# Attention stage of one core: VectorE's maxima, scale chain and half differences of the next head pair stand in other thirds of its ticks

## The chip, the cores and the metric

The kernel runs on one core of one Trainium2 chip, as one launch. The metric is the device time of a launch in microseconds (us); the kernel before takes 2028.98 us, the median of three runs.

## What is computed

Block-causal attention over q, k, v of shape (4, 8, 576, 64), then a mixture of eight experts, then a gated layer:

```python
scores = scale * np.matmul(q, k.transpose(0, 1, 3, 2))
mask = (pos // 64)[:, None] >= (pos // 64)[None, :]
attn = softmax(np.where(mask, scores, -1e9))
x = np.matmul(attn, v)            # then to (2304, 512)
# 8 rounds of row and column scaling of exp(x @ w_gate) give P
x = sum(P[:, e:e+1] * (np.maximum(x @ w1[e], 0) @ w2[e]) for e in range(8))
out = (silu(x @ wg) * (x @ wv)) @ wo
```

All is float32 on the outside. Inside, an operand is scaled by a power of two and cut into two float16 halves, a high one and the difference that is left, so that a product is made of float16 matmuls.

## The kernel before, in words

Two heads make a pair; there are 16 pairs p (four batches of four), and the work of a pair is cut into eight ticks u = 0 to 7 (`NTK`, `TICKS`, L824 to L827), in which the score rows of one, or two, blocks of 64 queries are made. `attention` (L833) is a generator. One pass of its loop (L1216) is one tick tk = 8p + u, and it yields three times, so that a tick has three thirds; between them the caller (L1417) puts in other work at fixed rates: the first two experts' weights (`w0`, in the first part of the stage), and, once the first batch is through, `fill`, which is router, expert products and their evacuation.

- Third 0: the events of the tick (below), then the scores' matmuls of the tick (`scores`, L989), in a PSUM bank of a pool of three.
- Third 1: the transposes of tick tk-4 (L1067, L1076), pending sums of x (`work`), the reciprocals of tick tk-2 (`normalise`, L1034 to L1039, after which GpSimd scales the rows, L1044), and VectorE's row maxima of the tick's own scores (`maxima`, L1002).
- Third 2: ScalarE's exponentials of tick tk-1 (`exps`, L1019).

The order is written out by hand: each engine executes in the order in which this loop issues, and tiles carry the semaphores. A next pair is prepared by events, a table from tick to functions (`at`, L1174). With r = 8p the first tick of pair p, and i = 0 for q, 1 for k, the pairs from 4 on have:

- `load_qk` (L907): SP's load of q or k into the tile `qk0` or `qk1`, at r-14 and r-13. Each has one buffer, which `lo_qk` of the pair before is the last to read.
- `max_qk` (L920): VectorE's maximum (L923), r-11 and r-10; after k's, two products that make `qk_d` (L103).
- `across_mid` (L106) at r-8: a matmul that spreads the maxima over the partitions into a bank that it shares with the scores of tick u = 0.
- `scale_qk` (L929) at r-7: VectorE's read of that bank (L116), and then the chain of the scales: L156, L163, L164 and two of L934.
- `hi_qk` (L937): ScalarE's high half (L940), r-6 and r-4; `lo_qk` (L942): VectorE's difference (L944), which reads that half, r-5 and r-4, and behind each on SP four transfers that put the halves into the scores' layout (`st`, L955 and L957).

The maxima of v for the next batch (`scan_max`, L883) are VectorE events too, one per pair. In each tick all these events stand in third 0, ahead of the tick's reciprocals and row maxima.

Of the kernel before, what the change touches and what calls it, by code (L numbers as in the profile page):

```python
# [30 lines left out]
def attention_moe_glu_kernel(  # L31
# [66 lines left out]
    def across_begin(mx, n, name):  # L98
        pool = pairs[0] if name[0] in "qv" else small
        tag = "dgw" if name[0] == "w" else f"dg{n}"  # L100
        d = pool.tile([P, n, P], F32, tag=tag, name=f"{name}_d", bufs=1)
        for i in range(n):
            nc.vector.tensor_scalar_mul(d[:, i], ident, mx[:, i : i + 1])  # L103
        return {"d": d, "n": n, "name": name}

    def across_mid(g):  # L106
        bank, g["free"] = spread[0](g["name"])
        n = g["n"]
        g["row"] = bank[:, : n * P].rearrange("p (n q) -> p n q", n=n)
        nc.tensor.matmul(  # L110
            bank[:, : n * P], ones, g["d"].rearrange("p n q -> p (n q)"), start=True, stop=True
        )

    def across_end(g):
        r = small.tile([P, g["n"]], F32, tag=f"sr{g['n']}", name=f"{g['name']}_r")
        nc.vector.tensor_reduce(r, g["row"], axis=AX.X, op=ALU.max)  # L116
        g["free"]()
        row_out[0] = False
        return r
# [23 lines left out]

        return made

    def pow2_end(g, n, top, name, root=False, s=None, inv=None):

        given[0] += 340
        r = across_end(g)
        e = small.tile([P, n], F32, tag=f"se{n}", name=f"{name}_e")  # L150
        if root:
            nc.vector.tensor_scalar(
                e.bitcast(I32), r.bitcast(I32), 1, EXPONENT, op0=ALU.logical_shift_right, op1=ALU.bitwise_and
            )
        else:
            nc.vector.tensor_single_scalar(e.bitcast(I32), r.bitcast(I32), EXPONENT, op=ALU.bitwise_and)  # L156
        if inv is None:
            inv = small.tile([P, n], F32, tag=f"si{n}", name=f"{name}_i")
        if s is None:
            s = small.tile([P, n], F32, tag=f"ss{n}", name=f"{name}_s")  # L160
        up = 64 if root else 0
        least = 2.0 ** ((-50 if root else -100) - top)
        nc.vector.tensor_scalar(inv, e, 2.0 ** (up - top), least, op0=ALU.mult, op1=ALU.max)  # L163
        nc.vector.reciprocal(s, inv)  # L164
        return s, inv
# [661 lines left out]
    NTK = len(TICKS)  # L827
    ORDER = (0, 2, 1, 3)
# [4 lines left out]
    def attention(actx):  # L833
# [17 lines left out]
        vs, vmx, vt, qk, st, et, xf = {}, {}, {}, {}, {}, {}, {}  # L851
# [11 lines left out]
        def where(p):  # L863
            return p // NPAIR, ORDER[p % NPAIR]
# [3 lines left out]
        def load_v(b, hp, tag, bufs=1):  # L868
            t = tag
            if isinstance(tag, str):  # L870
                t = ap.tile([P, NJ, P], F32, tag=tag, name=f"{tag}_{b}_{hp}", bufs=bufs)
            cols = slice(hp * P, (hp + 1) * P)
            nc.gpsimd.memset(t[S - nf * P :, nf], 0.0)
            nc.sync.dma_start(t[:, :nf], v[b, : nf * P, cols].rearrange("(j p) d -> p j d", p=P))
            nc.sync.dma_start(t[: S - nf * P, nf], v[b, nf * P :, cols])
            return t
# [43 lines left out]
        def max_qk(p, i):  # L920
# [5 lines left out]
            if i == 1:  # L926
                st[p]["m"] = across_begin(st[p]["m"], 2, f"qk{p}")

        def scale_qk(p):  # L929
            s, iv = pow2_end(st[p]["m"], 2, 11, f"qk{p}")  # L930
            sc = small.tile([P, 2], F32, tag="sc", name=f"sc_{p}")
            for i in range(2):
                f = (1 - 2 * i) * D**-0.5
                nc.vector.tensor_scalar(sc[:, i : i + 1], iv[:, 0:1], iv[:, 1:2], f, op0=ALU.mult, op1=ALU.mult)  # L934
            st[p].update(sc=sc[:, 0:1], nsc=sc[:, 1:2], s=s)
# [143 lines left out]
        def rest(p):  # L1079

            t = ps_x.tile([P, 512], F32, tag="x", name=f"t_{p}_r").rearrange("p (j q) -> p j q", q=P)
            return self_transpose(p, NC - 1, 4, t)

        def values(p, grp):
            g = st[p]
            c0, c1 = (0, 4) if grp == 0 else (4, NC)
            a = g["a0"] if grp == 0 else g["a1"]
            nj = (c1 + 1) // 2
            n = (c1 - c0) * CB
            x = ps_x.tile([P, 512], F32, tag="x", name=f"x_{p}_{grp}")[:, :n]  # L1090
            for j in range(nj):
                f = max(c0, 2 * j)
                for h in range(2):
                    nc.tensor.matmul(
                        x[h * D : (h + 1) * D, (f - c0) * CB : n],
                        vt[p][:, j, h * D : (h + 1) * D],
                        a[:, j, f - c0 : c1 - c0, h * CB : (h + 1) * CB],
                        start=j == 0,
                        stop=j == nj - 1,
                    )  # L1100
            return x
# [59 lines left out]
        def work(n):  # L1161
            for _ in range(min(n, len(pend))):
                pend.popleft()()

        def hurried():
            if hurry[0]:
                work(1)
                hurry[0] -= 1
                if not hurry[0]:
                    ready[0] += S // 2  # L1170

        events = {}

        def at(tick, f, *a):  # L1174
            events.setdefault(tick, []).append(lambda: f(*a))

        for p in range(1, npairs):
            r = p * NTK
            if p < DIRECT:
                if p > 1:  # L1180
                    at(r - NTK, load_direct, p)
                    at(r - 2, lambda p: vt.update({p: load_v(*where(p), "v", 2)}), p)
                continue
            for i in range(2):
                if p > 1:
                    at(r - 14 + 1 * i, load_qk, p, i)
                at(r - 11 + i, max_qk, p, i)
                at(r - 6 + 2 * i, hi_qk, p, i)
                at(r - 5 + 1 * i, lo_qk, p, i)
            at(r - 8, lambda p: across_mid(st[p]["m"]), p)  # L1190
            at(r - 7, scale_qk, p)
            at(r - 2, lambda p: vt.update({p: load_v(*where(p), "v", 2)}), p)
        for b in range(B):
            r = (b - 1) * NPAIR * NTK
            for i in range(NPAIR):
                if b:
                    at(r + i * NTK + (0 if i else 3), scan_load, b, i)
                at(r + i * NTK + NTK if b else 1 + i, scan_max, b, i if b else ORDER[i])
            r = r + NPAIR * NTK if b else NPAIR
            at(r, scale_v_begin, b)  # L1200
            at(r + (2 if b else 1), lambda b: across_mid(vmx[b]), b)
            at(r + (3 if b else 2), scale_v_end, b)
# [10 lines left out]
        def on(k):  # L1213
            return 0 <= k < tot

        for tk in range(tot + NTK):  # L1216
            p, u = divmod(tk, NTK)
            calm[0] = 0 < u < 5
            here[0] = (p, u) if on(tk) else None
            for f in events.pop(tk, ()):  # L1220
                f()
            here[0] = None
            if on(tk):
                scores(p, u)
            if u == 6 and p < npairs:
                take(p, 0, values(p, 0))
            hurried()
            yield
            out1 = None
            if on(tk - 4):  # L1230
                out1 = transposes(*divmod(tk - 4, NTK))
            if hurry[0]:
                hurried()
            else:
                work(2 if len(pend) > 6 else 1)
            if on(tk - 2):
                normalise(*divmod(tk - 2, NTK))
            if out1:
                out1()
            if on(tk):  # L1240
                maxima(p, u)
            yield

            if p and u == 4:
                work(len(pend))
                take(p - 1, 1, values(p - 1, 1))
                st.pop(p - 1)
                vt.pop(p - 1)
                if p == npairs:
                    work(len(pend))  # L1250
                    ready[0] = B * S // 2
                elif p % NPAIR == 0:
                    hurry[0] = len(pend)
            if p and u == 3:
                rest(p - 1)()
            if on(tk - 1):
                exps(*divmod(tk - 1, NTK))
            if u != 4:
                hurried()
            yield  # L1260


# [619 lines left out]
```

## Time and profile before

| what | us |
|---|---|
| median of three runs | 2028.98 |
| lowest run | 2028.92 |
| profiled execution, its own time | 2025.01 |
| span of its trace, first to last instruction | 2023.2 |

All numbers of the trace come from the one profiled execution. "Busy" counts an engine's instructions from start to end; PE is TensorE's matmuls, PEld its weight loads, DVE is VectorE, ACT is ScalarE, POOL is GpSimd and SPq the queue of SyncE, from which most transfers are issued. A row of the timeline has a start, a length, the engine, the line, what is written and read, a count (rows of equal instructions are merged), and in square brackets how long the engine was idle before it and what ended that. Tick ends are read off VectorE's rows of L1002, whose last part is a `DVE_READ_ACCUMULATOR2`. Attention with its fill stands in about the first 340 us of the span.

### The profile page before, as it was taken

To read this page: it belongs to the slowest core of one execution; us is meant where nothing else is said; L and a number is where in the kernel's file an instruction comes from. 1 tells how busy PE (TensorE), PEld (TensorE's weight loads), DVE (VectorE), ACT (ScalarE), POOL (GpSimd) and SP (SyncE) were. 2 spreads that over 40 slices of the span, in tenths; PEclk is the share of its full clock that TensorE was granted. 3 is DMA by queue.
4 is the path that set the end of the run, shared out by engine and by line. 5 is a ranking of instruction groups with operands and counts; after the bars stand their busy time and mean duration, and the time that the engine had idled before them with its cause. 6 is when DMAs were issued, how large, how long until landed. Compare 5 with 4: busy or idle time off the path is not lost. (4 is left out here: it accounts for less than half of the span.)

```text
span 2023.2 us, 47049 instructions
## 1 busy us (share of the span) xinstructions
PE 1940.9 (96%) x18378; PEld 1669.3 (83%) x18378; DVE 1593.5 (79%) x3404; ACT 1383.8 (68%) x2880; POOL 622.4 (31%) x876
## 2 busy tenths in 40 slices
PE   8789999999999999989999999999999889999998
PEld 4457677889888988878888888898889778888987
DVE  8886774888889788798978889778886887667666
ACT  6766775477777788777877877778776656544443
POOL 5544444013333333333333333333332132000000
PEclk9899999999999999999999999999999999999999
DMA  5334331326777786777767767677686100301111
GB/s 154 110 104 116 112 89 39 131 59 134 154 170 165 147 171 129 168 154 162 171 133 166 158 136 176 132 165 158 143 178 152 38 12 17 95 1 53 33 43 53
DMA packets 168079, 236.72 MB, mean 117 GB/s; under 512 B 16432, under 2 KB 84656, under 8 KB 167856
## 3 DMA queue, kind: packets, MB, share of 16 engines
q0 software_dynamic: 67136, 108.29, 31.0%
q1 hardware_dynamic: 100720, 125.42, 19.6%
q8 instruction: 144, 2.36, 0.5%
q14 instruction: 79, 0.65, 0.1%
HBM read 90.39 MB, written 24.38 MB: 57 GB/s over the span
## 5 line engine op out<-in xcount | busy, mean ns | idle before, releaser
L548 PEld LDWEIGHTS <-w 128*128 128x128 f16 x6720 | 609.3, 98 | 81.1 <-issue 17.5
L658 PEld LDWEIGHTS <-m_h 128*128 128x128 f16 x5292 | 512.9, 98 | 69.5 <-issue 6.7
L1537 POOL DMA_DIRECT2D acc<-ev x354 | 311.9, 928 | 577.3 <-ACT ev L1541 393.4
L548 PE MATMUL abc_m_b<-xs,w 128*128 128x256 f16 (+1 forms) x3840 | 474.9, 263 | 7.8 <-ACT m_t L575 4.8
L658 PE MATMUL m_o_b<-w,m_h 128*128 128x256 f16 x3024 | 403.3, 273 | 9.8 <-ACT ev L1541 6.0
L658 PE MATMUL m_o_ac<-w,m_h 128*128 128x256 f16 x2268 | 309.4, 273 | 0.0
L548 PE MATMUL abc_m_c<-xs,w 128*128 128x256 f16 (+1 forms) x1920 | 227.7, 263 | 0.0
L1541 ACT ACTIVATE ev<-m_o_b,pe 128x256 f32<-128x256 f32 x354 | 163.8, 479 | 66.7 <-PE m_o_b L658 45.4
L1541 ACT ACTIVATE ev<-m_o_ac,pe 128x256 f32<-128x256 f32 x236 | 136.3, 581 | 45.2 <-PE m_o_ac L658 43.8
L183 DVE SCALAR_TENSOR_TENSOR w<-wr,ws,w 128x512 f16<-128x512 f32 x210 | 156.0, 752 | 8.3 <-ACT w L179 8.3
L179 ACT ACTIVATE w<-wr,ws 128x512 f16<-128x512 f32 x210 | 150.1, 724 | 16.5 <-DVE ws L164 11.4
L194 DVE TENSOR_TENSOR m_h<-m_t,m_h 128x512 f16<-128x512 f32 x189 | 129.5, 687 | 32.4 <-ACT m_h L696 31.5
L696 ACT CAST m_h<-m_t 128x512 f16<-128x512 f32 x189 | 117.1, 619 | 29.1 <-DVE m_t L720 28.0
L689 ACT ACTIVATE m_h<-m_t 128x512 f16<-128x512 f32 x189 | 118.3, 626 | 23.0 <-DVE m_t L587 14.9
L548 PEld LDWEIGHTS <-gg_w 128*128 128x128 f16 x1260 | 114.4, 98 | 22.0 <-issue 10.0
L693 DVE SCALAR_TENSOR_TENSOR m_h<-m_t,m_h 128x512 f16<-128x512 f32 x189 | 128.6, 685 | 3.1 <-ACT m_h L689 2.8
L1524 POOL DMA_DIRECT2D acc<-ev_s x52 | 62.5, 1201 | 218.8 <-ACT ev_s L1517 214.1
L548 PEld LDWEIGHTS <-gv_w 128*128 128x128 f16 x1260 | 113.9, 98 | 15.1 <-issue 3.5
L658 PEld LDWEIGHTS <-g_h 128*128 128x128 f16 x1134 | 111.6, 99 | 16.3 <-issue 2.3
L1044 POOL TENSOR_SCALAR e<-e,r 128x64 f32<-128x64 f32 (+2 forms) x144 | 85.0, 597 | 118.5 <-DVE r L1039 78.7
L548 PE MATMUL abc_m_a<-xs,w 128*128 128x256 f16 (+1 forms) x960 | 118.5, 263 | 0.0
L572 DVE TENSOR_TENSOR m_t<-m_t,abc_m_b 128x512 f32<-128x512 f32 x73 | 49.4, 677 | 68.3 <-PE abc_m_b L548 60.3
(320 smaller groups left out, 3393.4 us busy)
## 6 DMA issues: line engine op xcount, KB each, us to landing
acc<-ev POOLq DMA_DIRECT2D x354, 256.0 KB, 4.1
wr<-in_w_dram SPq DMA_DIRECT2D x128, 256.0 KB, 5.5
acc<-ev_s POOLq DMA_DIRECT2D x52, 256.0 KB, 3.9
st<-hl SPq DMA_DIRECT2D x48, 144.0 KB, 3.5
raw_g<-in_w_gate_dram SPq DMA_DIRECT2D x12, 512.0 KB, 4.8
raw_v<-in_w_val_dram SPq DMA_DIRECT2D x12, 512.0 KB, 5.1
raw_o<-in_w_out_dram SPq DMA_DIRECT2D x12, 512.0 KB, 5.0
scr_g<-gg SPq DMA_DIRECT2D x21, 256.0 KB, 3.4
```

Of the source, the lines that this page charges most:

```text
L179: nc.scalar.activation(hi, src, AF.Copy, scale=s)
L183: nc.vector.scalar_tensor_tensor(lo, src, s, hi, op0=ALU.mult, op1=ALU.subtract)
L194: nc.vector.tensor_sub(lo, src, hi)
L548: nc.tensor.matmul(ps[:, f, to : to + w], W[o][:, sh, k, f * P : (f + 1) * P], xs[:, o, mh, k, c0 : c0 + w], start=x not in begun, stop=Tr ...
L658: nc.tensor.matmul(ps, h[o][:, sh, k, ii * P : (ii + 1) * P], W[o][:, mh, k], start=o in (X11, X12) and k == 0 and j == 0, stop=True, skip ...
L689: nc.scalar.activation(hi, src, AF.Relu)
L693: nc.vector.scalar_tensor_tensor(lo, src, 0.0, hi, op0=ALU.max, op1=ALU.subtract)
L696: nc.scalar.copy(hi, src)
L1044: nc.gpsimd.tensor_scalar(et[c][:, :n], et[c][:, :n], g["r"][:, c : c + 1], 1.0, op0=ALU.mult, op1=ALU.mult)
L1524: nc.gpsimd.dma_start(acc[:, x - 1 : x + 1, cols], e, accum_op=ALU.add)
L1537: nc.gpsimd.dma_start(acc[:, x], e, accum_op=ALU.add)
L1541: nc.scalar.activation(e[:, cols], ps, AF.Copy, scale=p)
```

## The change

The table of events gets thirds: `at` takes a third, and events of third 2 are issued at a tick's end, behind the exponentials and the fill of that third. Of each pair from 4 on, the two loads go from r-14 and r-13 to r-12 and r-11; the two maxima stay in r-11 and r-10 but go to third 2; the read of the spread maxima stays at r-7, and the chain that follows it goes to r-6; the high half of q goes from r-6 to r-5 (that of k stays at r-4); the two differences stay in r-5 and r-4 but go to third 2. The maxima of v go from third 0 of a pair's first tick to third 2 of the last tick of the pair before. No instruction is added or removed. The order of TensorE and of GpSimd is the same, that of ScalarE differs by 12 moved instructions, VectorE's and SP's differ only in the attention stage.

```diff
-    def pow2_end(g, n, top, name, root=False, s=None, inv=None):
+    def pow2_end(g, n, top, name, root=False, s=None, inv=None, r=None):
 
         given[0] += 340
-        r = across_end(g)
+        if r is None:
+            r = across_end(g)
...
+        def read_qk(p):
+            st[p]["row"] = across_end(st[p]["m"])
+
         def scale_qk(p):
-            s, iv = pow2_end(st[p]["m"], 2, 11, f"qk{p}")
+            s, iv = pow2_end(None, 2, 11, f"qk{p}", r=st[p]["row"])
...
-                if p > 1:
-                    at(r - 14 + 1 * i, load_qk, p, i)
-                at(r - 11 + i, max_qk, p, i)
-                at(r - 6 + 2 * i, hi_qk, p, i)
-                at(r - 5 + 1 * i, lo_qk, p, i)
+                at(r - 12 + i, load_qk, p, i)
+                at(r - 11 + i, max_qk, p, i, third=2)
+                at(r - 5 + i, hi_qk, p, i)
+                at(r - 5 + i, lo_qk, p, i, third=2)
             at(r - 8, lambda p: across_mid(st[p]["m"]), p)
-            at(r - 7, scale_qk, p)
+            at(r - 7, read_qk, p)
+            at(r - 6, scale_qk, p)
...
-                at(r + i * NTK + NTK if b else 1 + i, scan_max, b, i if b else ORDER[i])
+                at(r + i * NTK + NTK - 1 if b else 1 + i, scan_max, b, i if b else ORDER[i], third=2 if b else 0)
...
-            for f in events.pop(tk, ()):
-                f()
+            run(tk, 0)
...
             if u != 4:
                 hurried()
+            run(tk, 2)
             yield
```

Three places show it. The first is VectorE in tick u = 1 of pair 6: `qk7_r`, `_e`, `_i`, `_s` and `sc_7` are the read and the chain for pair 7, `r_5` the reciprocals of pair 5's last tick, `junk` with `bias` the row maxima of pair 6. Before:

```order
L116 TENSOR_REDUCE qk7_r_1640<-qk7_a_1592 128x2
L156 TENSOR_SCALAR qk7_e_1642<-qk7_r_1640 128x2
L163 TENSOR_SCALAR qk7_i_1644<-qk7_e_1642 128x2
L164 RECIPROCAL qk7_s_1645<-qk7_i_1644 128x2
L934 TENSOR_SCALAR sc_7_1648<-qk7_i_1644 128x1 x2
L377 TENSOR_REDUCE wmx_1_1_1478<-wr_1_1_11_1476 128x1
L383 TENSOR_REDUCE wm1_1_1_1661<-wmx_1_1_1478 128x1
L103 TENSOR_SCALAR w11_d_1663<-ident_72,wm1_1_1_1661 128x128
L194 TENSOR_TENSOR xs_79<-xf1_5_0_1532,xs_79 128x128
L1034 TENSOR_SCALAR r_5_1270<-sum_5_1269 128x1
L1039 RECIPROCAL r_5_1270<-r_5_1270 128x1
```

and now, from four rows behind the same read on:

```order
L195 TENSOR_TENSOR xs_79<-xf1_5_0_1528,xs_79 128x128
L1038 TENSOR_SCALAR r_5_1270<-sum_5_1269 128x1
L1043 RECIPROCAL r_5_1270<-r_5_1270 128x1
L1006 ISA junk_126,bias_6_1599<-s_6_1_1642,zero_127,sc_6_1352 128x192
L1006 ISA bias_6_1599 128x1
L1006 ISA junk_126,bias_6_1599<-s_6_1_1642,zero_127,sc_6_1352 128x256
L1006 ISA bias_6_1599 128x1
L780 SCALAR_TENSOR_TENSOR m0_0_h10_1636<-abc_m0_0_b_1279,m0_0_h10_1636 128x512
L157 TENSOR_SCALAR qk7_e_1680<-qk7_r_1640 128x2
L164 TENSOR_SCALAR qk7_i_1682<-qk7_e_1680 128x2
L165 RECIPROCAL qk7_s_1683<-qk7_i_1682 128x2
L938 TENSOR_SCALAR sc_7_1686<-qk7_i_1682 128x1 x2
```

The chain for pair 7 has gone from ahead of the reciprocals and the row maxima of the tick to behind them.

The second place is VectorE in ticks u = 3 and 4 of pair 5, where `hl0_6` and `hl1_6` are the differences of q and k for pair 6, and `w0_1_3` and `m0_0_t0` are fill. Before:

```order
L944 SCALAR_TENSOR_TENSOR hl0_6_1355<-qk0_6_1018,qk6_s_1313,hl0_6_1355 128x576
L1038 TENSOR_SCALAR r_5_1270<-sum_5_1269 128x2
L1039 RECIPROCAL r_5_1270<-r_5_1270 128x2
L1002 ISA junk_126,bias_5_1268<-s_5_3_1397,zero_127,sc_5_982 128x384
L1002 ISA bias_5_1268 128x1
L183 SCALAR_TENSOR_TENSOR w0_1_3_1377<-wr_1_0_10_888,ws_1_0_1125,w0_1_3_1377 128x512
L944 SCALAR_TENSOR_TENSOR hl1_6_1426<-qk1_6_1042,qk6_s_1313,hl1_6_1426 128x576
L1038 TENSOR_SCALAR r_5_1270<-sum_5_1269 128x1
L1039 RECIPROCAL r_5_1270<-r_5_1270 128x1
L1002 ISA junk_126,bias_5_1268<-s_5_4_1434,zero_127,sc_5_982 128x448
```

and now:

```order
L1006 ISA junk_126,bias_5_1268<-s_5_3_1387,zero_127,sc_5_1013 128x384
L1006 ISA bias_5_1268 128x1
L184 SCALAR_TENSOR_TENSOR w0_1_3_1373<-wr_1_0_10_886,ws_1_0_1123,w0_1_3_1373 128x512
L948 SCALAR_TENSOR_TENSOR hl0_6_1385<-qk0_6_1084,qk6_s_1349,hl0_6_1385 128x576
L1042 TENSOR_SCALAR r_5_1270<-sum_5_1269 128x1
L1043 RECIPROCAL r_5_1270<-r_5_1270 128x1
L1006 ISA junk_126,bias_5_1268<-s_5_4_1426,zero_127,sc_5_1013 128x448
L1006 ISA bias_5_1268 128x1
L948 SCALAR_TENSOR_TENSOR hl1_6_1422<-qk1_6_1130,qk6_s_1349,hl1_6_1422 128x576
```

Each difference stands behind the row maxima of its tick (384 and 448 wide) instead of ahead of them.

The third place is SP's queue over the same ticks: `qk0_7` and `qk1_7` are the loads of q and k for pair 7, `st0_6` and `st1_6` the four transfers each of pair 6's halves, `wr` the loads of expert weights. Before:

```order
L910 DMA qk0_7_1357<-in_qT_dram 128x576
L955 DMA st0_6_1390<-hl0_6_1355 64x576 x4
L910 DMA qk1_7_1395<-in_kT_dram 128x576
L957 DMA st1_6_1429<-hl1_6_1426 64x1152 x4
L372 DMA wr_1_1_00_1470<-in_w2_dram 128x2x256
```

and now:

```order
L959 DMA st0_6_1417<-hl0_6_1385 64x576 x4
L911 DMA qk0_7_1424<-in_qT_dram 128x576
L961 DMA st1_6_1463<-hl1_6_1422 64x1152 x4
L373 DMA wr_1_1_00_1468<-in_w2_dram 128x2x256
L373 DMA wr_1_1_01_1470<-in_w2_dram 128x2x256
L373 DMA wr_1_1_10_1472<-in_w2_dram 128x2x256
L373 DMA wr_1_1_11_1474<-in_w2_dram 128x2x256
L911 DMA qk1_7_1486<-in_kT_dram 128x576
```

Each load has gone from ahead of the four transfers that share its tick to behind them, and k's for pair 7 also behind four loads of weights.

## Rows read from the trace of the kernel before

**Rows 1.** The page's first part: busy time, share of the span, instructions.

```profile
span 2023.2 us, 47049 instructions
PE 1940.9 (96%) x18378; PEld 1669.3 (83%) x18378; DVE 1593.5 (79%) x3404; ACT 1383.8 (68%) x2880; POOL 622.4 (31%) x876
```

**Rows 2.** Stretches: length, PE, PEld, DVE, ACT, POOL busy, clock, DMA share, GB/s.

```profile
60.00:160.00 100.00, 83.71 (x664) 53.33 (x661) 82.84 (x275) 67.78 (x175) 48.69 (x100) 0.88 0.42 120
160.00:215.00 55.00, 54.47 (x525) 39.59 (x524) 40.79 (x155) 38.08 (x103) 25.38 (x61) 1.00 0.37 107
215.00:240.00 25.00, 21.83 (x196) 15.30 (x194) 19.80 (x69) 19.19 (x53) 13.41 (x29) 1.00 0.31 85
240.00:310.00 70.00, 69.32 (x653) 49.58 (x651) 48.76 (x184) 48.03 (x128) 32.27 (x73) 1.00 0.37 103
```

**Rows 3.** Waits, 60 to 340 us: waiter, releaser, us in total, times, longest.

```profile
DVE hl L944 <- ACT hl L940: 17.1, 9, 3.8
PE s L989 <- ACT e L1019: 8.4, 8, 2.6
PE t L1076 <- POOL e L1044: 6.1, 3, 2.3
```

**Rows 4.** Timeline, tick u = 1 of pairs 6 and 7.

```profile
120.67 0.17 DVE L156 TENSOR_SCALAR qk_e<-qk_r 128x2 int32<-128x2 int32 x1
...
121.39 0.68 DVE L377 TENSOR_REDUCE wmx<-wr 128x1 f32<-128x512 f32 x1
...
123.28 0.74 POOL L1044 TENSOR_SCALAR e<-e,r 128x576 f32<-128x576 f32 x1 [4.77 <-DVE r L1039]
...
124.08 0.66 PE L1076 MATMUL t<-ident,e 128*128 128x128 f32 x4 [1.90 <-POOL e L1044]
...
145.83 0.23 DVE L156 TENSOR_SCALAR qk_e<-qk_r 128x2 int32<-128x2 int32 x1
...
146.86 0.68 DVE L587 TENSOR_TENSOR m_t<-m_t,abc_m_c 128x512 f32<-128x512 f32 x1
...
149.56 0.52 PE L989 MATMUL s<-st,st 128*64 128x384 f16 x4 [2.63 <-ACT e L1019]
```

**Rows 5.** Timeline, tick u = 4 of pair 6: the halves of k.

```profile
127.88 0.81 ACT L940 ACTIVATE hl<-qk,qk_s 128x576 f16<-128x576 f32 x1
...
128.73 0.82 DVE L944 SCALAR_TENSOR_TENSOR hl<-qk,qk_s,hl 128x576 f16<-128x576 f32 x1 [1.51 <-ACT hl L940]
```

**Rows 6.** Timeline of VectorE, ends of ticks u = 3 and 5 of pair 3.

```profile
60.55 0.08 DVE L1002 DVE_READ_ACCUMULATOR2_ANT bias<- 128x1 f32 x1
...
65.79 0.09 DVE L1002 DVE_READ_ACCUMULATOR2_ANT bias<- 128x1 f32 x1
```

**Rows 7.** Timeline of VectorE and SP, ticks u = 3 to 6 of pair 5.

```profile
104.10 0.08 DVE L1002 DVE_READ_ACCUMULATOR2_ANT bias<- 128x1 f32 x1
104.10 0.75 DVE L183 SCALAR_TENSOR_TENSOR w<-wr,ws,w 128x512 f16<-128x512 f32 x1
...
107.91 2.39 SPq L957 DMA_DIRECT2D st<-hl  x4
...
110.25 0.09 DVE L1002 DVE_READ_ACCUMULATOR2_ANT bias<- 128x1 f32 x1
110.34 2.20 SPq L372 DMA_DIRECT2D wr<-in_w_dram  x4
...
111.21 0.75 DVE L923 TENSOR_REDUCE qm<-qk 128x1 f32<-128x576 f32 x1 [0.88 <-DMA qk<-in_kT_dram]
111.88 0.48 DVE L103 TENSOR_SCALAR qk_d<-ident,qm 128x128 f32<-128x128 f32 x2
...
114.16 0.08 DVE L1002 DVE_READ_ACCUMULATOR2_ANT bias<- 128x1 f32 x1
```

**Rows 8.** Transfers, 60 to 340 us: KB each, median us from issue to landing.

```profile
qk<-in_kT_dram SPq DMA_DIRECT2D x11, 288.0 KB, 3.4
...
qk<-in_qT_dram SPq DMA_DIRECT2D x10, 288.0 KB, 3.0
```

More of the change, by code (lines that the diff above doesn't have):

```diff
@@ L1172, in attention, with at, run @@
         events = {}
-        def at(tick, f, *a):
-            events.setdefault(tick, []).append(lambda: f(*a))
+        def at(tick, f, *a, third=0):
+            events.setdefault((tick, third), []).append(lambda: f(*a))
+        def run(tick, third):
+            for f in events.pop((tick, third), ()):
+                f()
         for p in range(1, npairs):
```

## The prediction

> **What bounds the kernel now.** I read the page's first part, then the busy times by stretch, then the waits, then the timeline around the pairs' first and middle ticks. The page says that TensorE is busy for 96% of the span [rows 1]; a change that adds and removes no instruction can gain only where TensorE stands. All moved instructions lie in the attention stage, the first 340 us, so I cut that stage into stretches [rows 2]. From 160 to 215 and from 240 to 310 us TensorE idles 0.53 and 0.68 us: there it sets the pace, and VectorE, busy for 74% and 70%, has room to be late. From 60 to 160 us TensorE idles 100 - 83.71 = 16.3 us and is granted a clock of 0.88, VectorE is busy for 83%; from 215 to 240 us TensorE idles 25 - 21.83 = 3.2 us. So what the change can give lies in 19.5 us of idle time, 1% of the launch, and a little clock. Two per cent, 40.6 us, is about what a measurement of this kernel can tell from no change.
>
> The waits say what that idle time hangs on [rows 3]: scores that wait for a bank which ScalarE's exponentials free (8.4 us in eight), transposes that wait for rows which GpSimd scales (6.1 us in three). VectorE itself waits 17.1 us, in nine pieces, for ScalarE's high half of k.
>
> **The change, part by part.**
>
> *The chain leaves tick 1.* In tick 1 of pair 6, TensorE idles 1.90 us for GpSimd, and GpSimd has idled 4.77 us for VectorE's reciprocals [rows 4]. VectorE is busy from instruction to instruction ahead of them, and the chain occupies it from 120.67 until the next instruction starts at 121.39, 0.72 us. Behind the row maxima it no longer delays these reciprocals: they, GpSimd and TensorE come 0.72 us earlier. The three waits of this kind give 3 x 0.72 = 2.2 us. In pair 7 the chain takes 146.86 - 145.83 = 1.03 us and delays a sum that ScalarE needs before it frees the bank for which TensorE idles 2.63 us; I count two such waits of the eight, 2 x 1.03 = 2.1 us. Together 4.3 us. From below it is worth nothing, if the work that now stands in tick 2 delays what follows as much; from above, all of the 14.5 us of the two waits.
>
> *The differences go behind the row maxima.* The 1.51 us that VectorE stands before k's difference [rows 5] is filled: reciprocals and row maxima of tick 4 go first, while ScalarE makes the half. Nine such waits are 17.1 us, but only the first is in the stretch that VectorE paces with nothing else in its way; behind 150 us TensorE hides nearly all of it. I take one, 1.5 us; the bounds are 0 and 17.1.
>
> *The loads come later.* This is the cost. Before, SP issued a load as soon as the difference that read its buffer was done, ahead of the four transfers of that tick; now it stands behind them. Four transfers take 2.39 us to issue [rows 7], a load of q lands 3.0 us after its issue, one of k 3.4 [rows 8]. So q's maximum can start 2.4 + 3.0 = 5.4 us after q's difference ends. VectorE's way there, for pair 7: from the end of tick 3 (104.18) to the end of tick 5 (110.34) it took 6.16 us; the difference (0.82) [rows 5] joins and the maximum (0.75) leaves, 6.23; the fill (0.75) and the difference itself stand ahead of the point from which I count, so 6.23 - 0.75 - 0.82 = 4.66 us. It waits 0.7 us. For k: the transfers of k start when q's load is issued (0.4), take 2.4, so 2.4 + 0.4 + 2.4 = 5.2; here four loads of weights (2.20) stand ahead too, 7.4; landing at 10.8. VectorE comes there at 4.66 + 0.7 + 0.75 (maximum of q), plus tick 6, which took 114.24 - 110.34 = 3.9 with a wait of 0.88, the maximum 0.75 and the products 0.48 that leave it, so 1.8: 7.9 in all. It waits 2.9 us; the 0.88 that it waited before goes. For pair 5, from 60.63 to 65.88 us, 5.25 us [rows 6], the same sum gives 5.25 + 0.07 - 0.82 = 4.5, a wait of 0.9 for q, and 5.2 + 3.4 = 8.6 against 4.5 + 0.9 + 0.75 + some 1.0 for a short tick 6 = 7.1, a wait of 1.5 for k. Sum of the two pairs: 0.7 + 2.9 - 0.88 + 0.9 + 1.5 = 5.1 us; pair 6, whose ticks are longer, I put at 1. Behind a waiting maximum stand the products for the spread, the next tick's reciprocals and row maxima, and so GpSimd and ScalarE. VectorE idles for 17% of that stretch already, so a part of the 6.1 us falls on idle time: I take 4.0. The bounds are 0, and 12 us if five pairs (four to 160 us, one at 215 to 240 us) wait 1.2 us at each of two loads and all of it arrives.
>
> The Trainium skill speaks against this part: "DMA: Bandwidth & Descriptors", Rules for kernel authors, tells one to issue a transfer early and to wait for its semaphore late. By the same page's section Anatomy of one DMA, a transfer costs about 2.0 us plus its bytes at 436 GB/s; for 288 KB I estimate 2.7 us from it, so that by the page each load would land 0.3 to 0.7 us sooner than the rows have it and the waits of pairs 5 and 7 would come to about 3 us instead of 5.1. That fit was made on transfers of another queue; the trace's 3.0 and 3.4 us stand.
>
> *The rest.* ScalarE's high half of q moves by one tick together with the chain that it waits for, the maxima of v by one third; both stay beside work of other engines, at nothing. SP no longer stands with a load whose buffer is in use, so stores behind it go earlier; no row shows that anyone on TensorE's path waits for them, 0 again. The halves of q reach the scores' layout two thirds of a tick later, with three ticks to go; bounds 0 and 1 us, I take 0.
>
> Sum: -4.3 - 1.5 + 4.0 = -1.8 us on the profiled execution's 2025.0, so 2023.2. The median shown is 2028.98, 4.0 us above that execution; on its scale the forecast is 2027.2.
>
> **The rivals.**
>
> *VectorE's ticks become even, and TensorE stops waiting.* From 60 to 160 us the idle 16.3 us go, as they are gone behind 160 us: 2029.0 - 16.3 = 2012.7. For it: every large wait of TensorE that I opened stands in the first ticks of a pair, where the moved work stood. Against it: VectorE is busy for 83% there, its work stays, and loads come later. The granted clock of 0.88 in that stretch [rows 2] lies between 1.2 and 2.4 GHz because the chip drops to the lower level for part of it; full clock would give at most another 0.12 x 100 = 12 us. The Trainium skill ("Perfetto Trace Analysis", Matmul Optimizations) says that TensorE's power follows its utilization and asks for matmuls back to back; by that rule the two gains come together, 2001, and the trace agrees as far as the stretch with idle time is the one with the lower clock. I give this rival 0.2.
>
> *The maxima wait for their loads and the ticks stretch.* Place: the end of ticks 5 and 6. It decides from the point where VectorE needs less than 5.4 us from q's difference to q's maximum, that is, from two ticks of under 5.4 + 0.82 - 0.07 = 6.15 us, which both pairs above are at or below. Price: the 12 us of the upper bound, with none of the two gains: 2041. For it: k's load already came too late once, by 0.88 us, with the old lead [rows 7]. Against it: VectorE idles there anyway. I give it 0.2.
>
> *TensorE's pace hides all of it.* The waits go and come on engines with room, 2029. For it: the two long stretches with under 1 us of idle time. 0.2.
>
> **How the numbers follow.** The forecast has 0.4 (its own range 2021 to 2035), the rivals 0.2 each. I predict 2027.2. The range goes from 2014, where most of the first rival is in, to 2041, the second. Faster by over 2% needs all idle time, all the clock and more: 0.02. Slower by over 2% needs more than three times the upper bound of the loads: 0.03. Within 2%: 0.95.
>
> **What would show it.** Right: the nine waits of L944 for L940 gone; transposes' waits for GpSimd in tick 1 shorter by about 0.7 us; L923 waiting for both loads, 0.7 to 3 us each, early in the stage, and longest for pair 7's k. Wrong: no waits at L923 (the loads land sooner than I sum), TensorE's idle time from 60 to 160 us under 5 us or over 25, or a changed time behind 340 us, where the order is the same.

## The result and the profile after

The changed kernel takes 2038.36 us, median of five runs, against 2028.98 us for the kernel before, of which two more runs were made: ratio 1.0059, 95% interval 1.0046 to 1.0071. The ratio compares the fast runs of both, so it leaves out one run of the kernel before that took 4270.53 us; the quotient of the two medians alone is 1.0046. The prediction was 2027.2 us with a range of 2014 to 2041. The time is in the range, on the side of the rival of the late loads, and it is a small loss where a small gain was forecast. Lines below about L820 stand one further down in the changed kernel, later ones four to eight: the maxima are L924, the high halves L944, the differences L948, the scores L993, the exponentials L1023.

The page's first part after, for [rows 1]: the busy times are within 5 us of before's, and the span is 15.7 us longer (this execution is 2.4 us above its median, the one of before 4.0 below its own). Of these 15.7 us, 5.0 are in TensorE's busy time and 10.7 in its idle time.

```profile
span 2038.9 us, 47049 instructions
...
PE 1945.9 (95%) x18378; PEld 1671.4 (82%) x18378; DVE 1593.1 (78%) x3404; ACT 1382.4 (68%) x2880; POOL 622.7 (31%) x876
```

The stretches after, for [rows 2], in the same columns:

```profile
60.00:160.00 100.00, 74.74 (x591) 46.87 (x588) 78.11 (x265) 64.59 (x171) 45.28 (x94) 0.88 0.37 105
160.00:215.00 55.00, 53.38 (x508) 38.75 (x507) 36.95 (x133) 34.50 (x92) 26.68 (x61) 1.00 0.40 114
215.00:240.00 25.00, 23.08 (x205) 15.57 (x202) 18.65 (x66) 19.85 (x53) 10.99 (x24) 1.00 0.42 116
240.00:310.00 70.00, 66.31 (x625) 47.91 (x626) 49.82 (x182) 44.05 (x117) 33.00 (x71) 1.00 0.34 97
```

TensorE's idle time from 60 to 160 us is 100 - 74.74 = 25.3 us against 16.3, at the same granted clock of 0.88. In the other three stretches it is 1.6, 1.9 and 3.7 us against 0.5, 3.2 and 0.7. Together 32.5 - 20.7 = 11.8 us more, about 0.6% of the launch. Windows of one length do not hold the same work, though: from 60 to 160 us there are 591 matmul records after and 664 before. VectorE, the engine that was moved, is less busy from 60 to 160 us (78.11 against 82.84 us), so it waits more too.

TensorE's instructions stand in the same order in both traces, so a late matmul can be matched with itself. The last product with v of the attention stage, before and after:

```profile
348.95 2.28 PE L1094 MATMUL x<-a,v 128*64 128x320 f32 x20
```

```profile
361.99 2.27 PE L1098 MATMUL x<-a,v 128*64 128x320 f32 x20
```

At this point, called the stage's end below, the changed kernel is 13.0 us late. The other 2.7 of the span's 15.7 us come behind it, where nothing was moved; there the traces of the runs below differ by up to 4.9 us among themselves, so no cause is read from them.

Who waits for whom, 60 to 350 us, in the columns of [rows 3], first TensorE:

```profile
PE qk_a L110 <- DVE qk_d L103: 10.2, 4, 5.6
PE abc_qk L110 <- DVE r L1042: 4.8, 1, 4.8
PE qk_a L110 <- DVE r L1042: 3.6, 4, 1.1
PE s L993 <- ACT e L1023: 3.4, 6, 0.8
```

and VectorE:

```profile
DVE qm L924 <- DMA qk<-in_kT_dram: 9.3, 6, 4.0
...
DVE qm L924 <- DMA qk<-in_qT_dram: 5.4, 4, 2.2
```

The first three rows were not among before's waits at all: the matmul that spreads the maxima over the partitions (L110, in `across_mid`) waits 18.6 us for VectorE. (The reciprocal `r` that the second and third row name stands behind the products `qk_d` on VectorE; the matmul reads `qk_d`, and in each of these waits it starts 0.06 us after `qk_d` ends.) Scores that wait for exponentials fell from 8.4 us to 3.4. Not all of that is a gain: in x3 below, where no spread matmul waits, they still wait 5.9. VectorE's maxima wait 14.7 us for their loads.

How the two are tied can be seen in pair 5, where the maxima of pair 7 are made. VectorE, TensorE and SP's queue there, for [rows 7]:

```profile
109.68 1.03 DVE L948 SCALAR_TENSOR_TENSOR hl<-qk,qk_s,hl 128x576 f16<-128x576 f32 x1
...
112.55 0.58 SPq L911 DMA_DIRECT2D qk<-in_qT_dram  x1
...
113.23 2.38 SPq L961 DMA_DIRECT2D st<-hl  x4
...
113.74 0.09 DVE L1006 DVE_READ_ACCUMULATOR2_ANT bias<- 128x1 f32 x1
...
115.65 2.16 SPq L373 DMA_DIRECT2D wr<-in_w_dram  x4
...
116.00 0.75 DVE L924 TENSOR_REDUCE qm<-qk 128x1 f32<-128x576 f32 x1 [2.18 <-DMA qk<-in_qT_dram]
...
117.86 0.47 SPq L911 DMA_DIRECT2D qk<-in_kT_dram  x1
...
122.65 0.75 DVE L924 TENSOR_REDUCE qm<-qk 128x1 f32<-128x576 f32 x1 [4.01 <-DMA qk<-in_kT_dram]
123.32 0.47 DVE L103 TENSOR_SCALAR qk_d<-ident,qm 128x128 f32<-128x128 f32 x2
...
123.85 1.22 PE L110 MATMUL qk_a<-qk_d,ones 128*128 128x256 f32 x2 [5.64 <-DVE qk_d L103]
```

The load of k leaves behind eight transfers, at 117.86, and lands at about 122.6; VectorE idles 4.01 us at its maximum, and TensorE, which has nothing to do with loads of q and k, idles 5.64 us at the spread matmul behind it. Before, in the same place, k's maximum waited 0.88 us, its products ended at 111.88 + 0.48 = 112.36 [rows 7], and the spread matmul ran at 113.92 without a wait. Before's timeline of both engines, with a wait of VectorE ahead of q's maximum of pair 7, and the products and spread matmuls of pair 5 (made in pair 3's ticks), pair 7 and pair 9:

```profile
66.47 0.80 DVE L103 TENSOR_SCALAR qk_d<-ident,qm 128x128 f32<-128x128 f32 x2
...
68.40 0.60 PE L110 MATMUL abc_qk<-qk_d,ones 128*128 128x256 f32 x2
...
108.07 0.69 DVE L581 TENSOR_TENSOR m_t<-m_t,abc_m_a 128x512 f32<-128x512 f32 x1 [1.42 <-PE abc_m_a L548]
...
113.92 0.60 PE L110 MATMUL qk_a<-qk_d,ones 128*128 128x256 f32 x2
...
161.87 0.75 DVE L103 TENSOR_SCALAR qk_d<-ident,qm 128x128 f32<-128x128 f32 x2
...
167.38 0.60 PE L110 MATMUL qk_a<-qk_d,ones 128*128 128x256 f32 x2
```

The products had 113.92 - 112.36 = 1.56 us in hand for pair 7, 68.40 - 67.27 = 1.13 us for pair 5, and 167.38 - 162.62 = 4.76 us for pair 9. The change moves the maximum by two thirds of a tick, and two ticks of pair 5 took 6.16 us [rows 7]: about 2 us by this estimate. The twelve spread matmuls from pair 4 on bear it out. Ten had 0.7 to 3.8 us in hand before and all ten wait after the change; pairs 9 and 13, with 4.8 us, are the two that do not.

### The profile page after: what moved, and what is told of

Same layout as the page of the kernel before. It is cut to its first block, busy times and chain, and to the rows that moved or that the text cites. A ratio compares the mean times of both kernels' runs of the same rounds, so it can differ in the third digit from the quotient of the medians.

```text
span 2038.9 us, 47049 instructions
## 1 busy us (share of the span) xinstructions
PE 1945.9 (95%) x18378; PEld 1671.4 (82%) x18378; DVE 1593.1 (78%) x3404; ACT 1382.4 (68%) x2880; POOL 622.7 (31%) x876
```

## The experiments

All were timed in five rounds beside the kernel before on the same chip; a ratio is to that, which took 2028.74 us beside the x runs, 2026.84 beside y1 to y3 and z1, 2026.99 beside y4, w1, w2 and z2, and 2026.91 beside the h runs. The last column is how much later than in the kernel before the stage's end comes, in the one profiled execution of each; where nothing was moved (y3) it is 0.5 us, and h2 and h3, equal in time, differ by 1.6, so less than that says nothing. "Two buffers" means `bufs=2` for the tiles `qk0` and `qk1`, so that a load need not wait for the difference before; `NZ0, NZ1` go from 34, 14 to 32, 16 to make room. In the edits, `-` is the kernel named as the base.

| label | base and edit | median us | ratio, 95% interval | stage's end, us |
|---|---|---|---|---|
| after | the changed kernel | 2038.36 | 1.0059 (1.0046 to 1.0071) | 13.0 |
| x1_loads_back | after, loads where they were | 2036.71 | 1.0037 (1.0024 to 1.0051) | 11.2 |
| x2_two_buffers | after, two buffers, loads at r-14 and r-13 | 2034.79 | 1.0031 (1.0020 to 1.0043) | 7.2 |
| x3_two_buffers_max_first | x2, maxima in third 0 | 2023.86 | 0.9972 (0.9963 to 0.9981) | -4.0 |
| x4_max_last | before, maxima in third 2 | 2035.31 | 1.0033 (1.0020 to 1.0046) | 8.6 |
| z1_max_last_earlier | x2, maxima one tick earlier | 2021.72 | 0.9968 (0.9955 to 0.9981) | -4.0 |
| z2_max_later | x2, maxima one tick later | 2054.55 | 1.0135 (1.0115 to 1.0156) | 29.8 |
| y1_chain_only | before, chain at a tick's end | 2028.78 | 1.0000 (0.9989 to 1.0011) | 0.3 |
| y2_lo_only | before, two buffers, differences in third 2 | 2027.86 | 1.0000 (0.9990 to 1.0011) | -0.3 |
| y3_two_buffers_alone | before, two buffers | 2028.46 | 0.9997 (0.9986 to 1.0009) | 0.5 |
| y4_v_only | before, maxima of v moved | 2027.23 | 1.0002 (0.9992 to 1.0012) | 1.3 |
| w1_x3_v_back | x3, maxima of v put back | 2024.56 | 0.9987 (0.9978 to 0.9997) | -4.1 |
| w2_chain_and_lo | y1 and y2 together | 2027.18 | 1.0005 (0.9995 to 1.0015) | 0.4 |
| h1_lo_and_hi | y2, high half of q later | 2030.55 | 1.0010 (0.9998 to 1.0022) | -0.2 |
| h2_chain_lo_hi | w2, high half of q later | 2023.30 | 0.9979 (0.9967 to 0.9990) | -2.5 |
| h3_chain_lo_hi_v | h2, maxima of v moved | 2023.27 | 0.9982 (0.9973 to 0.9991) | -4.1 |

**Where the loss comes from: loads or places.** T is the theory that the loss is the loads' lateness, as the prediction's rival has it; P that it is the place of the maxima at the tick's end. In x1 the loads go back ahead of the transfers:

```diff
-                at(r - 12 + i, load_qk, p, i)
+                at(r - 14 + i, load_qk, p, i, third=2 * i)
```

> The changed kernel with the loads of q and k issued where they were before, each as soon as the difference that reads its buffer is done and ahead of that tick's four transfers. Theory T (late loads): VectorE's maxima wait for loads that now stand behind the transfers, the products for the spread come late, and TensorE's spread matmul, which executes in order, waits for them. Then the waits of L924 for loads fall from 14.7 us to under 4, those of the spread matmul L110 for qk_d from 18.6 us to under 6, and the time is 2024 to 2032 us. Rival P (late place): the maxima at a tick's end are late enough by themselves, since TensorE runs ahead of VectorE. Then the spread matmul keeps at least 12 us of waits and the time stays at 2034 to 2040 us.

Its maxima hardly wait (1.6 and 0.4 us), but two thirds of the loss stay, and so do spread matmuls that wait: 8.1 us, between T's figure and P's. Its waits, 60 to 350 us:

```profile
PE qk_a L110 <- DVE r L1042: 3.3, 4, 1.1
PE qk_a L110 <- DVE qk_d L103: 2.7, 3, 1.3
...
PE abc_qk L110 <- DVE r L1042: 2.1, 1, 2.1
...
DVE qm L924 <- DMA qk<-in_kT_dram: 1.6, 2, 1.2
...
DVE qm L924 <- DMA qk<-in_qT_dram: 0.4, 1, 0.4
```

x2 takes the loads out of the question, and x3 then undoes the maxima's place alone:

```diff
-        ap.tile([P, S], F32, tag=f"qk{i}", name=f"qk{i}_{p}")
+        ap.tile([P, S], F32, tag=f"qk{i}", name=f"qk{i}_{p}", bufs=2)
-                at(r - 12 + i, load_qk, p, i)
+                at(r - 14 + i, load_qk, p, i)
...
-                at(r - 11 + i, max_qk, p, i, third=2)
+                at(r - 11 + i, max_qk, p, i)
```

> The changed kernel with two buffers each for q and k and the loads issued at r-14 and r-13, so that no load waits for a reader (two of the float16 places are given up in this stage for the space). T: no wait of L924 for a load, spread matmul's waits under 5 us, 2022 to 2031 us. P: as in the first run, at least 12 us of waits at the spread matmul and 2034 to 2040 us.

> As the run with two buffers, and the maxima back in third 0 of their ticks; what is left of the change is the chain, the high half of q, the differences and the maxima of v. Both T and P: the spread matmul's waits are as before the change (none over 1 us), and what the prediction counted as gains (4.3 + 1.5 us) stands alone: 2020 to 2026 us. If these gains were nothing: 2027 to 2031 us.

The last pair of lines is x3's alone. In x2 no maximum waits for a load, its spread matmuls wait 7.3 us behind 36 us, and it is still slower than before; in x3 no spread matmul waits for VectorE, and it is faster than before. The 7.3 us are again fewer than P's 12 and more than T's 5; the times are P's. x2's waits from 60 to 350 us (the 1.4 us missing from the 7.3 are pair 4's, ahead of that):

```profile
PE qk_a L110 <- DVE r L1042: 3.5, 4, 1.1
...
PE qk_a L110 <- DVE qk_d L103: 2.4, 4, 1.3
```

x4 does the maxima's move alone, on the kernel before, whose line numbers it keeps up to L1172:

```diff
-                at(r - 11 + i, max_qk, p, i)
+                at(r - 11 + i, max_qk, p, i, third=2)
```

> The kernel before with the maxima of q and k alone moved to third 2 of their ticks; the loads, the chain, the halves and the maxima of v stay. T: the loads have their old lead, so the maxima wait for none, and the time is within 3 us of the kernel before. P: the spread matmul waits for the late products at most pairs' starts, 8 us or more in all, and the kernel is 5 to 12 us slower than before.

```profile
PE qk_a L110 <- DVE r L1038: 3.5, 4, 1.1
...
PE qk_a L110 <- DVE qk_d L103: 1.5, 2, 1.3
...
PE abc_qk L110 <- DVE r L1038: 0.5, 1, 0.5
```

The ratio is 1.0033, with loads that stand where they stood and no maximum that waits for one: this is P. And x3 says that what is left of the change, with its maxima early, is a gain. At the stage's end the parts add up: -4.01 us for what x3 keeps, 11.18 for the maxima's place (x2 less x3) and 5.87 for the loads (the changed kernel less x2), 13.04 together.

**Place or distance.** z1 and z2 keep the maxima at a tick's end and move them by a tick, away from the spread matmul of r-8 or up to it:

```diff
-                at(r - 11 + i, max_qk, p, i, third=2)
+                at(r - 12 + i, max_qk, p, i, third=2)
```

In z2 the new line has `r - 10 + i`.

> The changed kernel with two buffers, the loads at r-14 and r-13, and the maxima in third 2 of one tick earlier, r-12 and r-11: still at a tick's end, but further ahead of the spread matmul than before the change. P1 (what costs is the distance to the spread matmul): its waits for qk_d under 2 us, 2018 to 2026 us. P2 (what costs is the tick's end itself, by what then stands behind the maxima): 2031 to 2037 us, as with the maxima at the end of r-11 and r-10.

> The version with two buffers (2034.8 us, 1.0031; its spread matmuls wait 7.3 us behind 36 us), with only the maxima of q and k one tick later, in the last third of ticks r-10 and r-9, so that the spread matmul of tick r-8 comes straight behind the products of k's maximum. P, the distance from the maximum to the spread matmul is what costs: a tick less of it, some 4 us for each of the pairs in the stretch that VectorE paces, so the spread matmuls wait 20 to 50 us in all and the time is 2045 to 2075. Rival, VectorE is one stream and it is its work at the tick's end that costs: 2033 to 2037, as with the tick before.

z1 has no waiting spread matmul and, at 0.9968, the lowest median here, though x3 at 0.9972 cannot be told from it. z2's spread matmuls wait 21.9 us for VectorE behind 60 us (and 3.3 more that the list puts down to a load of v, though the matmul starts 0.05 us after its products), and it loses 27.6 us in the medians:

```profile
PE qk_a L110 <- DVE qk_d L103: 19.7, 7, 4.4
...
PE abc_qk L110 <- DVE qk_d L103: 2.2, 1, 2.2
```

So the end of a tick is as good a place as its start; what costs is too little time between the maximum and the matmul that needs it. The three distances, a tick apart, give 0.9968, 1.0031 and 1.0135.

**Where the gain comes from.** y1 does the predicted first gain alone, y2 the second; y3 is the control for the buffers, y4 the maxima of v:

```diff
-            at(r - 7, scale_qk, p)
+            at(r - 7, read_qk, p)
+            at(r - 7, scale_qk, p, third=2)
```

> The kernel before with the read of the spread maxima left where it is and only the scales' chain moved behind the reciprocals and row maxima of its tick (third 2 of tick 1); nothing else. Theory G1 (the chain is the gain): 2 to 6 us faster than before, the prediction's term being 4.3, and TensorE's waits at the first ticks of pairs shorter by about 0.7 us each. Rival G2 (the gain of the earlier run is elsewhere): within 1.5 us of before.

```diff
-                at(r - 5 + 1 * i, lo_qk, p, i)
+                at(r - 5 + 1 * i, lo_qk, p, i, third=2)
```

> The kernel before with the two differences moved to third 2 of their ticks, and two buffers each for q and k so that no load waits for them (two float16 places fewer in this stage). G1: the waits of VectorE for the half of k (17.1 us) go, the time falls by the prediction's 1.5 us, 0 to 3. G2: 4 to 6 us faster, and the whole gain is here.

> Control: the kernel before with two buffers each for q and k and two float16 places fewer, nothing moved. G1: within 1.5 us of before. Rival G3 (the gain of the run with two buffers and the maxima first came from the loads, not from the moved work): 3 to 6 us faster.

> The kernel before, with only the maxima of v moved, from the first third of a pair's first tick to the last third of the tick before it. Three theories on where the 5 to 6 us come from that the change keeps when its maxima of q and k stand early (two buffers, maxima in the first third: 0.9972). V, they come from the maxima of v, which leave the tick in which transposes wait for GpSimd: 2022 to 2025 us, and the eight scores that wait for the exponentials' bank (8.4 us) fall below 5. C, they need the chain and the differences together, since each alone gave what it won back at the next scores: 2027 to 2030 here, the waits of the scores for the exponentials within 2 us of before's. H, they come from the high half of q one tick later, with the chain a whole tick later: 2027 to 2030 here too.

None of the four moved the time clear of noise. y2 takes VectorE's 17.1 us of waiting for ScalarE's half down to 0.6 us and wins no time by it. y1's trace shows why the chain's gain does not last; its waits, 60 to 350 us:

```profile
PE s L993 <- ACT e L1023: 11.7, 11, 2.0
PE t L1080 <- POOL e L1048: 3.6, 3, 1.5
...
ACT hl L944 <- DVE qk_s L165: 7.9, 5, 2.6
```

The transposes wait 3.6 us for GpSimd instead of 6.1 [rows 3], as predicted, but the scores wait 11.7 us for exponentials instead of 8.4. The third row is new: ScalarE's high half of q stands at the head of tick r-6, right behind the chain that makes its scale. In y1's timeline, pair 6:

```profile
123.35 0.66 PE L1080 MATMUL t<-ident,e 128*128 128x128 f32 x4 [1.06 <-POOL e L1048]
...
124.15 0.17 DVE L165 RECIPROCAL qk_s<-qk_i 128x2 f32<-128x2 f32 x1
...
124.35 0.77 ACT L944 ACTIVATE hl<-qk,qk_s 128x576 f16<-128x576 f32 x1 [2.63 <-DVE qk_s L165]
...
125.54 0.50 ACT L1023 ACTIVATE e<-s,bias,sc 128x192 f32<-128x192 f32 x1
...
126.73 0.58 PE L993 MATMUL s<-st,st 128*64 128x448 f16 x2 [1.96 <-ACT e L1023]
```

The same scores before:

```profile
126.34 0.96 PE L989 MATMUL s<-st,st 128*64 128x448 f16 x4 [0.28 <-ACT e L1019]
```

TensorE's wait at the transposes is 1.06 us instead of 1.90 [rows 4], but the scores that run 3.4 us later stand 1.96 us for a bank instead of 0.28: ScalarE waited 2.63 us for the chain, and the exponentials that free the bank stand behind the half. w1 and w2 looked for a sum of parts:

> The version with two buffers and the maxima of q and k in the first third (2023.9 us, 0.9972), with only the maxima of v put back to where they stood before. V: 2027 to 2030 us, the gain gone. C and H: 2022 to 2025, the gain stays. A time half way, 2025 to 2027, would say that the gain is a sum of parts and V has a share.

> The kernel before with two buffers, the chain at the end of tick r-7, and the differences in the last third; loads, maxima of q, k and v and the high halves as before. C: 2022 to 2025 us, faster than the chain alone (1.0000) and the differences alone (1.0000), with the waits of the scores for the exponentials below 8 us instead of the 11.7 of the chain alone. V and H: 2027 to 2030, the waits of the scores at 8 to 12 us.

Chain and differences together, with the high half of q still at r-6, give nothing, and ScalarE still waits 7.9 us for the chain in w2. w1, which differs from w2 in the half's tick and in the chain by one third of a tick, stays faster than before. So the next three moved the half:

```diff
-                at(r - 6 + 2 * i, hi_qk, p, i)
+                at(r - 5 + i, hi_qk, p, i)
```

> The kernel before with two buffers, the differences in the last third, and the high half of q one tick later (r-5); chain, loads and all maxima as before. Theory H2: the chain's gain is real but is given back because ScalarE's high half of q stands right behind the chain and waits for its reciprocals (7.9 us in five, in both kernels with the chain at the end of tick r-7), so that the exponentials behind it come late for the bank; here the chain stands where it stood, so there is nothing to win: 2026 to 2029 us, scores waiting for exponentials 7 to 10 us. Rival R, the later half itself gives the gain, by taking 0.9 us of ScalarE out of tick r-6: 2022 to 2025, those waits below 7.

> The kernel with chain and differences moved together (2027.2 us, 1.0005), with only the high half of q one tick later (r-5). H2: ScalarE's 7.9 us of waiting for the chain's reciprocals go, scores wait for exponentials about 6 us instead of 11.1, and the time is 2022 to 2025.5, as in the version with the maxima of v put back (0.9987). Rival R2, what counts there is the chain in the next tick's first third instead of at the end of tick r-7: 2026 to 2029, no faster than before.

> The same with the maxima of v moved too. If v has a share of its own once the rest has moved (0.9972 with, 0.9987 without, measured apart): 1.5 to 3 us faster than the same without v, 2020 to 2023. If that difference was one of the two chips: within 1 us of it.

The later half without the chain's move gives nothing (h1, 1.0010, with a median just above H2's range); with the chain moved it gives 0.9979 (h2), on the same chip. That rules out R, and R2 too, since h2's chain stands at the end of tick r-7. In h2 ScalarE's half no longer waits for the chain, and the scores wait 7.2 us for exponentials instead of y1's 11.7:

```profile
PE s L993 <- ACT e L1023: 7.2, 7, 1.7
PE t L1080 <- POOL e L1048: 3.6, 3, 1.5
```

The same place in h2's timeline: the exponentials come 1.05 us behind the transposes' start, in y1 2.19, and TensorE waits 0.84 us at the scores where it waited 1.96. Transposes and scores together are 2.18 us before, 3.02 in y1 and 1.90 in h2.

```profile
123.93 0.65 PE L1080 MATMUL t<-ident,e 128*128 128x128 f32 x4 [1.06 <-POOL e L1048]
...
124.98 0.52 ACT L1023 ACTIVATE e<-s,bias,sc 128x192 f32<-128x192 f32 x1
...
126.19 0.57 PE L993 MATMUL s<-st,st 128*64 128x448 f16 x4 [0.84 <-ACT e L1023]
```

h3 and h2 are within 0.03 us: the maxima of v have no share that can be seen, and w1's distance from x3 was taken on two chips; their stage's ends are 0.1 us apart.

## Why the prediction was wrong

*What bounds the kernel.* Right as far as it went: 13.0 of the span's 15.7 us are there at the stage's end, and most of it is idle time of TensorE. (The 2% that it called the least a measurement can tell was far too coarse: the intervals here are about 0.1% to either side.) But the waits of before list only links that were already late. The spread matmul was the next one, with 1.56 us in hand for pair 7 [rows 7], 1.13 for pair 5. The prediction read `qk_d` and never compared its end with the matmul's start.

*The failed step* is the price of the maxima's move. The prediction treated it as a question of loads alone ("VectorE waits"), let part of the wait fall on VectorE's idle time, and named as waiting behind the maximum the products, the next tick's reciprocals, GpSimd and ScalarE. It did not name TensorE's own matmul of tick r-8, which TensorE executes in order: behind it stand scores that do not read that maximum. With loads that were never late, the place alone costs 0.33% on the kernel before (x4: 6.6 us in the medians) and 0.59% on the changed one (x2 against x3: 10.9 us). That term was zero in the sum and is its largest.

*The loads come later.* The mechanism was right and the size too small. Loads that lead by two buffers take 1.0059 to 1.0031, 0.28% or 5.7 us, where I took 4.0 from a sum of 6.1; the bounds of 0 and 12 hold it. The stage's end gives 5.9. The waits themselves are larger than the sum: for pair 7, 2.18 and 4.01 us against 0.7 and 2.9, for pair 6 2.14 in k's against 1 for both, for pair 5 2.25 and 1.51 against 0.9 and 1.5; 14.7 us in all instead of 6.1. For q of pair 7 the load's side of the sum held: its maximum started 116.00 - 110.71 = 5.3 us after the difference of q ended, where the sum has 5.4. VectorE's side did not: it was there 113.83 - 110.71 = 3.1 us after, not 4.66, since the 6.16 us that the sum started from held a wait of 1.42 us for a product of TensorE (the row at 108.07) that was gone after the change. For k, in the same ticks, its load left at 117.86 and its maximum started at 122.65, 4.8 us, where I had taken 3.4 us for a landing; it is the transfer that stood behind eight others. The Trainium skill's rule to issue early and wait late ("DMA: Bandwidth & Descriptors", Rules for kernel authors) pointed to the right side. The estimate of 2.7 us for a landing, worked out from the Trainium skill's same page (Anatomy of one DMA), would have made these waits shorter and is further from them than the rows of before were; put in at every place it gives 3.7 us for pairs 5 and 7, not the 3 of the prediction, since VectorE too comes to k's maximum 0.3 us sooner.

*The chain leaves tick 1: 4.3 us*, and *the differences: 1.5 us*. The sum of 5.8 us is near what the change keeps once its maxima are early (3.6 us in h3, 4.9 in x3), but not by the steps given. The 0.72 us at tick 1's transposes was nearly right (0.84 in y1, 1.90 to 1.06); that it lasts was wrong as long as ScalarE's half stands behind the chain, and the edit that makes it last, the half one tick later, is one that the prediction costed at nothing. The differences by themselves gave nothing (y2); whether the chain with the later half does without them was not tried.

*The rivals.* The rival of the late loads named the right side, nearly the time (2041), and the smaller part of the mechanism. The first rival, even ticks, fell: even z1, with the lowest median, leaves 15.4 us of idle time from 60 to 160 us. Its argument from the clock is not borne out either: idle time from 60 to 160 us rose from 16.3 to 25.3 us with the granted clock at 0.88 both times, and before, the stretch from 215 to 240 us idled 3.2 of 25 us at 1.00 [rows 2]. "TensorE's pace hides all" fell by the stretch from 240 to 310 us, where idle time went from 0.7 to 3.7 us although TensorE had been the pace-setter there.

*The signs.* Transposes' waits for GpSimd shorter: right, 6.1 to 1.3 us in all, though in x3, where no spread matmul waits, 4.1 stay. Waits of L948 for L944 down to 0.4 us: right. Waits of the maxima for loads, longest for pair 7's k: right. Idle time over 25 us from 60 to 160 us, named as a sign against the forecast: it came, at 25.3. A changed time behind 340 us, the other such sign, came with 2.7 us in the one trace, within what the runs scatter there.

*What stays open.* The place of the maxima costs more on the changed kernel (10.9 us) than on the one before (6.6), with about the same waits at the spread matmul (7.3 and 7.6 us behind 36 us). At the stage's end it is 11.2 and 8.6 us; the uncertainties of the two ratios just overlap, and no run says why they should differ. Why x1 is 4.0 us later than x2 at the stage's end, with the same places and 2.0 us of waits for loads, is open too; their ratios cannot be told apart.

## What to carry to other kernels

Before work is moved later on one engine, find every reader of its result, small matmuls on the bounding engine too, and read off the trace how long before its reader it is done; that time in hand is the budget of the move, and the list of waits before did not show it. Where a link is taken off one path, look at what stands directly behind it on the engine that reads it: the gain lasts only if that reader moves too. A move that changes several places is worth taking apart, since here a gain of 0.2 to 0.3% stood beside losses of 0.9% together, and z1 has the first without the second.

## What the runs showed of the hardware

In this kernel an engine with idle time was no cushion for a wait that a busier engine inherits. VectorE was busy for 78% of the stretch from 60 to 160 us, yet one 4.01 us wait for a load on it, with one of 2.18 us ahead of it, became 5.64 us on TensorE; in x2, with the loads early, the same matmul waits 0.67. And a transfer of 288 KB whose median landing was 3.0 to 3.4 us [rows 8] took 4.8 us from its issue to the start of its reader when eight others had been issued ahead of it.
